# Sums with v stationary and a moving, long row loads from SyncE, v stored with partitions outermost, and one softmax product on GpSimd

## The chip, the cores and the metric

The kernel runs on one core of a Trainium2 chip. The metric is device time in microseconds, the median of several executions. In the tables PE is TensorE (matmuls), PEld its weight loads, DVE is VectorE, ACT is ScalarE, POOL is GpSimd and SP is SyncE, which here only issues transfers. "q" behind an engine's name is its instruction queue. A name such as L369 is line 369 of the kernel before.

## The reference

Attention through 32 memory slots for each of 8 batches and 8 heads (576 positions, head size 64), then a mixture of depths over the joined heads:

```
a   = softmax(phi, axis=slots)                  # (8, 8, 576, 32)
k_m = einsum('bhsm,bhsd->bhmd', a, k)
v_m = einsum('bhsm,bhsd->bhmd', a, v)           # "the sums"
x   = softmax(q k_m^T / 8) v_m                  # (8, 576, 512), heads joined
scores = x @ w_gate
for b: the 128 rows with the highest score get
    x += sigmoid(score) * (relu(x @ w1) @ w2)   # w1 512x1024, w2 1024x512
```

Which rows are chosen depends on small differences of the scores. So the kernel computes the softmax over the slots and the sums for v with more precision than one pass gives: a and v are split into a part of high bits and a remainder (hi and lo, by masking the low 12 bits), and the products of all parts are summed.

## The kernel before

**Softmax.** `softmax(i, ch)` works on one group of four heads of one batch, slots on the partitions: tiles of 128 x 576. There are 16 groups. It is a long chain of VectorE instructions with ScalarE roundings between them: a polynomial and a quotient, each step as `fma`, which multiplies in two parts. `fma` (L214 to L223) is called four times a group. Its `low = val * rl` is L221, and its addition L222 reads `low`. At the end `keys` transposes a (L306), splits it (L312, L314), writes its parts `alo` and `ahi` to the DRAM tensor `aparts` (L320, eight transfers a group, issued by POOL; L326 then copies them inside DRAM so that they stand there twice), and multiplies it with k (L330).

**v.** `split_v(b)` loads v in pieces of 128 x 1152 (L282), splits them into `vhi` and the remainder in `vb` (L285, L287), and stores each part twice in the DRAM tensor `vparts` (L290, four transfers a piece, issued by POOL, two buffers of each tile).

**The sums.** `values(st)` handles two batches (a set; there are four). In chunks of T = 16 positions it loads rows of vparts and aparts into `v_rows` and `a_rows` (two buffers; L350 by SP, L356 half by SP and half by POOL). A row of a chunk in a_rows consists of pieces of 32 floats. For each position four matmuls follow (L369), one for each strip of 32 partitions, into four accumulators: a is stationary (32 x 64), v moves (128 columns). The sums are evicted by ScalarE (L378), and `centre` transposes them (L392) and evicts them again (L394).

**The rest.** `attention(b)`: scores, exponentials, the product with v_m (L524), scaling (L528), a row added on POOL (L531), the gate's score (L498 to L503), the output (L535), the ranking and a gather (L600). `ffn` does two products with w1 and w2 (L625, L635) and scatters rows (L641).

**Order.** Each engine works through its instructions in the order in which the program gives them. That order is made by a loop of turns at the end of the kernel: a turn advances the softmaxes by one `yield`, v by one on every second turn while both chains run, the sums by STEPS = 9 (one yield is two positions), the attentions by one each, and a feed-forward by one or two. Two softmax chains run side by side until groups 0 to 7 are done; groups 8 to 15 form one chain. The sums of a set start 8 turns after its four groups.

Of the kernel before, what the change touches and what calls it, by code (L numbers as in the profile page):

```python
# [20 lines left out]
P = 128  # L21
# [17 lines left out]
def kernel(  # L39
# [27 lines left out]
    SET = 2  # L67
    T = 16
    scale = 1.0 / Dh ** 0.5
# [112 lines left out]
    def softmax(i, ch):  # L182
# [3 lines left out]
        def t(name, dtype=F32):  # L186
            return ex.tile([P, S], dtype, name=name)
# [26 lines left out]
        def fma(val, h, c):  # L214


            lo, big, low = t("lo"), t("big"), t("low")
            stt(out=lo, in0=val, scalar=GRID, in1=h, op0=ALU.mult, op1=ALU.subtract)  # L218
            tt(out=big, in0=h, in1=rh, op=ALU.mult)
            tt(out=lo, in0=lo, in1=rh, op=ALU.mult)  # L220
            tt(out=low, in0=val, in1=rl, op=ALU.mult)  # L221
            tt(out=low, in0=low, in1=lo, op=ALU.add)  # L222
            stt(out=val, in0=big, scalar=c * UP, in1=low, op0=ALU.add, op1=ALU.add)  # L223
# [54 lines left out]
    def split_v(b):  # L278

        for u in range(2):  # L280
            vb = vio.tile([P, S * Dh * NPR // P], F32, name="vb")
            nc.sync.dma_start(out=vb, in_=v[b, u])  # L282
            yield
            hi = vio.tile([P, S * Dh * NPR // P], F32, name="vhi")
            nc.vector.tensor_single_scalar(hi.bitcast(I32), vb.bitcast(I32), -4096,  # L285
                                           op=ALU.bitwise_and)
            nc.vector.tensor_sub(vb, vb, hi)  # L287
            for vp, src in enumerate((vb, hi)):
                for ap in range(2):
                    nc.gpsimd.dma_start(  # L290
                        out=vparts[u, b, :, ap, vp].rearrange("g r s d -> g (r s d)")
                                                   .rearrange("g (p x) -> g p x", p=P // 2),
                        in_=src)
            yield
# [3 lines left out]
    def keys(i, ch):  # L298
        ex, (b, g) = exs[ch], groups[i]
        a = soft.pop(i)  # L300
        kb = ks.pop(i)
        aS = ex.tile([PT, NC, P], F32, name="aS")
        for c0 in range(0, NC, 3):
            tp = bank([PT, 3, P])
            for c in range(3):
                nc.tensor.transpose(out=tp[:, c], in_=a[:, (c0 + c) * PT:(c0 + c + 1) * PT],  # L306
                                    identity=ident)
            nc.scalar.activation(aS[:, c0:c0 + 3], tp, AF.Copy)  # L308
        yield
# [6 lines left out]
        last = i == len(groups) - 1  # L316
        for h in range(4):
            for part, src in enumerate((lo, hi)):
                for vp in range(2 if last else 1):
                    (nc.sync if vp else nc.gpsimd).dma_start(  # L320
                        out=aparts[h // 2, h % 2, b, g, part, vp].rearrange("(c p) m -> p c m", p=PT),
                        in_=src[:, :, h * M:(h + 1) * M])
# [18 lines left out]
    def values(st):  # L341

        b0 = st * SET

        def load(ch):
            ss = slice(ch * T, (ch + 1) * T)
            for u in range(2):
                nc.sync.dma_start(  # L350
                    out=v_rows[ch % 2][2 * u::4, u].rearrange("p s d -> p (s d)").bitcast(F32),
                    in_=vparts[u, b0:b0 + SET].rearrange("b g t w r s d -> (b g t w r) (s d)")
                        [:, ch * T * Dh:(ch + 1) * T * Dh])
            for r in range(2):
                for u in range(2):
                    (nc.sync, nc.gpsimd)[u].dma_start(  # L356
                        out=a_rows[ch % 2][4 * r + 2 * u::8, :, r].bitcast(F32),
                        in_=aparts[r, u, b0:b0 + SET].rearrange("b g t w s m -> (b g t w) s m")[:, ss])

        n = S // T  # L360
        load(0)
        for ch in range(n):
            if ch + 1 < n:
                load(ch + 1)
            vr, ar = v_rows[ch % 2], a_rows[ch % 2]
            for s in range(T):
                for i in range(2 * SET):
                    p = slice(i * 32, i * 32 + 32)
                    nc.tensor.matmul(out=accs[i][:2 * M, :P].rearrange("p (u d) -> p u d", d=Dh),  # L369
                                     lhsT=ar[p, s].rearrange("p r m -> p (r m)"), rhs=vr[p, :, s],  # L370
                                     start=(ch == 0 and s == 0), stop=(ch == n - 1 and s == T - 1))
                if s % 2:
                    yield
        for bb in range(SET):
            v_m[b0 + bb] = const.tile([P, P], F32, name=f"v_m{b0 + bb}")
            for g in range(2):
                half = slice(g * 2 * M, (g + 1) * 2 * M)
                nc.scalar.activation(v_m[b0 + bb][half], accs[2 * bb + g][:2 * M, :P], AF.Copy)  # L378

    mean = {}  # L380

    def centre(b):
# [199 lines left out]
    def gather(b, t):  # L582
# [14 lines left out]
        gr = work.tile([P, 1], F32, name="gr")  # L597
        nc.scalar.activation(gr[:n], ps[:n, 1:2], AF.Tanh, scale=0.5)
        xe = work.tile([P, D], F32, name="xe")
        nc.gpsimd.indirect_dma_start(  # L600
# [6 lines left out]
    def ffn(b, t):  # L607
# [26 lines left out]
        for f in range(KF):  # L634
            nc.tensor.matmul(out=ps[:n], lhsT=hT[:, f, :n], rhs=w2_sb[:, f],  # L635
                             start=(f == 0), stop=(f == KF - 1))
            yield
        ye = one.tile([P, D], F32, name="ye")
        nc.vector.scalar_tensor_tensor(out=ye[:n], in0=ps[:n], scalar=gr[:n], in1=xe[:n],
                                       op0=ALU.mult, op1=ALU.add)  # L640
        nc.gpsimd.indirect_dma_start(  # L641
            out=out_flat[:(b + 1) * S],
            out_offset=bass.IndirectOffsetOnAxis(ap=idx[:n, 0:1], axis=0),
            in_=ye[:n], in_offset=None)

# [79 lines left out]

    STEPS = 9
    late_consts()
# [5 lines left out]
    while True:  # L733
# [77 lines left out]
```

## Time and profile before

| | before |
|---|---|
| median of 3 (range) | 1350.65 us (1348.28 to 1356.15) |
| span of the profiled execution | 1360.9 us |
| PE, PEld busy | 674.4 us, 479.3 us |
| DVE, ACT, POOL busy | 763.0 us, 292.6 us, 434.9 us |
| transfers | 166.41 MB in 201,868 packets, 154,896 of them under 512 B |
| sums' matmuls (L369) | 9,216, busy 245.5 us, from 346 us to 1,245 us |
| row loads issued on POOL (L356) | 288, busy 161.6 us |

How to read the profile: a line of the waits names the engine and instruction that waited, then what ended the wait, then the total in us, the number of times and the longest. A line of the groups has the busy time, the mean of one in ns and, behind the second bar, the engine's idle time just before them. A line of the busy times by stretch starts with the stretch in us and its length, then the busy us (and instructions) of PE, PEld, DVE, ACT and POOL, and last the granted TensorE clock, the share of the DMA engines and GB/s. A line of the timeline has the start and the duration in us. A line of the DMA issues has the count, KB each and the median us from issue to landing.

### The profile page before, as it was taken

Reading aid. Unit: us, or ns where it says so; the run is one execution under the profiler, and the core shown is the slowest. Engines: PE = TensorE matmul, PEld = TensorE weight load, DVE = VectorE, ACT = ScalarE, POOL = GpSimd, SP = SyncE. Lnnn points to the kernel's source line nnn. Section 1 sums busy time; section 2 is a strip of 40 time slices with the busy share of each in tenths; the row PEclk is TensorE's granted clock in tenths of the full one; section 3 lists DMA queues with packets and bytes.
Section 4 is the critical chain, followed back from the end, with each engine's and each line's share of the span. In section 5 each row is a group of like instructions: output and inputs, shape, how many; then the busy total and the mean of one; then the engine's idle time right before and its main releaser. Section 6 shows DMA issues by size and latency. Waiting matters only on the chain.

```text
span 1360.9 us, 25950 instructions
## 1 busy us (share of the span) xinstructions
PE 674.4 (50%) x10746; PEld 479.3 (35%) x10746; DVE 763.0 (56%) x1307; ACT 292.6 (21%) x569; POOL 434.9 (32%) x671
## 2 busy tenths in 40 slices
PE   0202010100336562474765645877464887677976
PEld 0101010100335452353553424555342555544542
DVE  8865846474434478375775876764937433202740
ACT  2202212121011213221413330421313220102320
POOL 5222313131423342325243234325230344321320
PEclk9999999999755655567668767776767778678968
DMA  8566767676555553344435244335440544433110
GB/s 274 150 159 180 186 159 178 128 185 180 133 128 118 126 139 94 98 120 124 124 104 141 73 109 124 96 96 159 99 108 12 117 136 126 110 94 76 67 42 18
DMA packets 201868, 166.41 MB, mean 122 GB/s; under 512 B 154896, under 2 KB 165136, under 8 KB 201744
## 3 DMA queue, kind: packets, MB, share of 16 engines
q0 software_dynamic: 88288, 79.37, 23.7%
q1 hardware_dynamic: 113456, 85.30, 23.6%
q8 instruction: 88, 1.44, 0.4%
q14 instruction: 36, 0.29, 0.1%
HBM read 105.05 MB, written 68.16 MB: 127 GB/s over the span
## 4 chain that ended last, share of the span: by engine, by line
DMA 32%; DVE 24%; PE 23%; POOL 6%; SPq 6%; issue 5%; ACT 3%; DVEq 0%; POOLq 0%; ACTq 0%
DMA a_rows<-aparts 13%; DMA vparts<-vhi 9%; PE acc L369 8%; DMA vparts<-vb 4%; SPq L350 4%; PE bank L625 3%; PE bank L635 3%; DMA vb<-in_v 3%; POOL aparts L320 2%; SPq L356 2%; DMA aparts<-alo 2%; PE bank L524 2%; DVE low L222 2%; DVE low L221 1%; DVE lo L218 1%
## 5 line engine op out<-in xcount | busy, mean ns | idle before, releaser
L369 PE MATMUL acc<-v_rows,a_rows 32*64 32x128 f32 x9216 | 245.5, 273 | 290.9 <-DMA a_rows<-aparts 286.2
L369 PEld LDWEIGHTS acc<-v_rows,a_rows 32*64 32x64 f32 x9216 | 220.4, 182 | 370.9 <-issue 277.3
L356 POOL DMA_DIRECT2D a_rows<-aparts x288 | 161.6, 567 | 410.1 <-PE acc L369 386.2
L306 PE MATMUL bank<-ident,e 128*96 128x128 f32 x96 | 23.7, 416 | 230.8 <-DVE e L273 230.3
L330 PE MATMUL bank<-aS,kb 96*128 96x64 f32 x384 | 70.8, 368 | 76.3 <-ACT aS L308 76.3
L306 PEld LDWEIGHTS bank<-ident,e 128*96 128x96 f32 x96 | 16.7, 191 | 238.5 <-issue 183.6
L330 PEld LDWEIGHTS bank<-aS,kb 96*128 96x128 f32 x384 | 69.8, 281 | 83.9 <-ACT aS L308 78.4
L625 PE MATMUL bank<-w_sb,xeT 128*128 128x512 f32 x128 | 87.9, 796 | 3.9 <-ACT xeT L616 3.9
L320 POOL DMA_DIRECT2D aparts<-alo x64 | 47.6, 743 | 128.9 <-DVE alo L314 86.9
L635 PE MATMUL bank<-w_sb,hT 128*128 128x512 f32 x128 | 81.6, 750 | 0.0
L290 POOL DMA_DIRECT2D vparts<-vb x32 | 26.0, 818 | 154.6 <-DVE vb L287 154.6
L285 DVE TENSOR_SCALAR vhi<-vb 128x1152 int32<-128x1152 int32 x16 | 12.3, 772 | 99.2 <-DMA vb<-in_v 56.6
L524 PE MATMUL bank<-vbd,eT 128*128 128x256 f32 x160 | 64.4, 542 | 0.0
L218 DVE SCALAR_TENSOR_TENSOR lo<-num,vh 128x576 f32<-128x576 f32 x48 | 36.1, 751 | 50.0 <-ACT vh L177 35.2
L498 DVE TENSOR_TENSOR prod<-xj,wg 128x1024 f32<-128x1024 f32 (+1 forms) x24 | 25.1, 1044 | 68.9 <-POOL xj L531 68.9
L531 POOL TENSOR_TENSOR xj<-xj,mean 128x1024 f32<-128x1024 f32 (+1 forms) x24 | 48.6, 2024 | 35.1 <-DVE xj L528 34.6
L177 ACT ACTIVATE vh<-num 128x576 int16<-128x576 f32 x32 | 21.9, 683 | 139.6 <-DVE num L223 130.8
L222 DVE TENSOR_TENSOR low<-low,lo 128x576 f32<-128x576 f32 x64 | 48.5, 758 | 2.2
L320 POOL DMA_DIRECT2D aparts<-ahi x64 | 47.5, 742 | 5.7 <-DMA vparts<-vb 2.2
L220 DVE TENSOR_TENSOR lo<-lo,rh 128x576 f32<-128x576 f32 x64 | 48.0, 750 | 0.0
L528 DVE TENSOR_TENSOR xj<-bank,rd 128x512 f32<-128x512 f32 x40 | 27.4, 687 | 35.7 <-PE bank L524 35.1
L524 PEld LDWEIGHTS bank<-vbd,eT 128*128 128x128 f32 x160 | 37.0, 256 | 17.9 <-issue 13.2
(151 smaller groups left out, 1294.7 us busy)
## 6 DMA issues: line engine op xcount, KB each, us to landing
v_rows<-vparts SPq DMA_DIRECT2D x288, 128.0 KB, 3.1
vparts<-vb POOLq DMA_DIRECT2D x32, 576.0 KB, 18.4
vparts<-vhi POOLq DMA_DIRECT2D x32, 576.0 KB, 20.8
kb<-in_k SPq DMA_DIRECT2D x16, 576.0 KB, 5.8
vb<-in_v SPq DMA_DIRECT2D x16, 576.0 KB, 8.0
a_rows<-aparts SPq DMA_DIRECT2D x288, 32.0 KB, 2.8
a_rows<-aparts POOLq DMA_DIRECT2D x288, 32.0 KB, 2.7
qb<-in_qT SPq DMA_DIRECT2D x16, 576.0 KB, 5.5
```

The costliest lines, as they stand in the source:

```text
L218: stt(out=lo, in0=val, scalar=GRID, in1=h, op0=ALU.mult, op1=ALU.subtract)
L220: tt(out=lo, in0=lo, in1=rh, op=ALU.mult)
L222: tt(out=low, in0=low, in1=lo, op=ALU.add)
L320: (nc.sync if vp else nc.gpsimd).dma_start(out=aparts[h // 2, h % 2, b, g, part, vp].rearrange("(c p) m -> p c m", p=PT), in_=src[:, :, h ...
L330: nc.tensor.matmul(out=km[:, rr], lhsT=kb[:, c, rr * P:(rr + 1) * P], rhs=aS[:, c, rr * 2 * M:(rr + 1) * 2 * M], start=(c == 0), stop=(c = ...
L350: nc.sync.dma_start(out=v_rows[ch % 2][2 * u::4, u].rearrange("p s d -> p (s d)").bitcast(F32), in_=vparts[u, b0:b0 + SET].rearrange("b g ...
L356: (nc.sync, nc.gpsimd)[u].dma_start(out=a_rows[ch % 2][4 * r + 2 * u::8, :, r].bitcast(F32), in_=aparts[r, u, b0:b0 + SET].rearrange("b g ...
L369: nc.tensor.matmul(out=accs[i][:2 * M, :P].rearrange("p (u d) -> p u d", d=Dh), lhsT=ar[p, s].rearrange("p r m -> p (r m)"), rhs=vr[p, :, ...
L524: nc.tensor.matmul(out=o[:, g * 4 * Dh:(g + 1) * 4 * Dh], lhsT=eT[:, g, (c0 + c) * P:(c0 + c + 1) * P], rhs=vbd[b % 3][:, g], start=False, ...
L531: nc.gpsimd.tensor_add(x, x, row.unsqueeze(1).to_broadcast([P, cols, D]))
L625: nc.tensor.matmul(out=ps[:n], lhsT=xeT[:, d, :n], rhs=w1_sb[:, d, f0:f0 + 512], start=(d == 0), stop=(d == KD - 1))
L635: nc.tensor.matmul(out=ps[:n], lhsT=hT[:, f, :n], rhs=w2_sb[:, f], start=(f == 0), stop=(f == KF - 1))
```

## The change

The sums exchange the roles of their operands: v is stationary (32 x 64), a's four heads move (4 x 32 columns). All loads of rows are issued by SP, in chunks of T = 24, with one run of 6 KB or 3 KB on a row; the doubled rows of a are read twice from one copy, so that `aparts` and its copies in DRAM shrink. A transpose and an eviction in `centre` fall away. v is handled by groups and stored with the partitions as outermost dimension, in two transfers a piece. The product `low` of each `fma` and v's subtraction move to POOL. The feed-forward writes its result into `xe` in place, with three buffers. One yield in `keys`, after the product with k, goes, and the turns are set anew. The tiles `gr` and `xe` get three buffers as `idx` does.

```diff
-    T = 16
+    T = 24
-    v_rows = [rows.tile([P, 2, T, Dh], F32R, name=f"v_rows{i}") for i in range(2)]
-    a_rows = [rows.tile([P, T, 2, M], F32R, name=f"a_rows{i}") for i in range(2)]
+    v_rows = [rows.tile([P, T, Dh], F32R, name=f"v_rows{i}") for i in range(2)]
+    a_rows = [rows.tile([P, 4, T, M], F32R, name=f"a_rows{i}") for i in range(2)]
...
+            nc.gpsimd.tensor_tensor(out=low, in0=val, in1=rl, op=ALU.mult)
             stt(out=lo, in0=val, scalar=GRID, in1=h, op0=ALU.mult, op1=ALU.subtract)
+            tt(out=lo, in0=lo, in1=rh, op=ALU.mult)
             tt(out=big, in0=h, in1=rh, op=ALU.mult)
-            tt(out=lo, in0=lo, in1=rh, op=ALU.mult)
-            tt(out=low, in0=val, in1=rl, op=ALU.mult)
             tt(out=low, in0=low, in1=lo, op=ALU.add)
...
-            nc.vector.tensor_sub(vb, vb, hi)
+            nc.gpsimd.tensor_sub(vb, vb, hi)
+            yield
             for vp, src in enumerate((vb, hi)):
-                for ap in range(2):
-                    nc.gpsimd.dma_start(
-                        out=vparts[u, b, :, ap, vp].rearrange("g r s d -> g (r s d)")
-                                                   .rearrange("g (p x) -> g p x", p=P // 2),
-                        in_=src)
+                nc.gpsimd.dma_start(
+                    out=vparts[b, g, :, vp].rearrange("w r s d -> w (r s d)")
+                                           .rearrange("w (p x) -> p w x", p=P),
+                    in_=src.unsqueeze(1).to_broadcast([P, 2, 4 * S * Dh // P]))
...
-        for part in range(0 if last else 2):
-            copies = aparts.rearrange("r u b g t w s m -> b g t w (r u) (s m)")[b, g, part]
-            copies = copies.rearrange("w h (x y) -> w x h y", x=16)
-            nc.gpsimd.dma_start(out=copies[1], in_=copies[0])
+        for part, src in enumerate((lo, hi)):
+            for h in range(4):
+                nc.gpsimd.dma_start(
+                    out=aparts[h, b, g, part].rearrange("(c p) m -> p c m", p=PT),
+                    in_=src[:, :, h * M:(h + 1) * M])
...
-        yield
...
+            nc.sync.dma_start(
+                out=v_rows[ch % 2][0::2].rearrange("p s d -> p (s d)").bitcast(F32),
+                in_=vparts[b0:b0 + SET].rearrange("b g t w r s d -> (b g t w r) (s d)")
+                    [:, ch * T * Dh:(ch + 1) * T * Dh])
+            for h in range(4):
+                src = aparts[h, b0:b0 + SET].rearrange("b g t s m -> (b g t) (s m)")
+                src = src[:, ch * T * M:(ch + 1) * T * M]
                 nc.sync.dma_start(
-                    out=v_rows[ch % 2][2 * u::4, u].rearrange("p s d -> p (s d)").bitcast(F32),
-                    in_=vparts[u, b0:b0 + SET].rearrange("b g t w r s d -> (b g t w r) (s d)")
-                        [:, ch * T * Dh:(ch + 1) * T * Dh])
-            for r in range(2):
-                for u in range(2):
-                    (nc.sync, nc.gpsimd)[u].dma_start(
-                        out=a_rows[ch % 2][4 * r + 2 * u::8, :, r].bitcast(F32),
-                        in_=aparts[r, u, b0:b0 + SET].rearrange("b g t w s m -> (b g t w) s m")[:, ss])
+                    out=a_rows[ch % 2][2 * h::8, h].rearrange("p s m -> p (s m)").bitcast(F32),
+                    in_=src.unsqueeze(1).to_broadcast([4 * SET, 2, T * M]))
...
-                    nc.tensor.matmul(out=accs[i][:2 * M, :P].rearrange("p (u d) -> p u d", d=Dh),
-                                     lhsT=ar[p, s].rearrange("p r m -> p (r m)"), rhs=vr[p, :, s],
+                    nc.tensor.matmul(out=accs[i][:Dh, :P].rearrange("p (h m) -> p h m", m=M),
+                                     lhsT=vr[p, s], rhs=ar[p, :, s],
...
-        tp = bank([P, P])
-        nc.tensor.transpose(out=tp, in_=v_m[b], identity=ident)
-        vm = work.tile([P, NPR, M], F32, name="vmT")
-        nc.scalar.activation(vm.rearrange("p r m -> p (r m)"), tp, AF.Copy)
+        vm = v_m[b]
...
-        idx = work.tile([P, 1], I32, name="idx")
+        idx = work.tile([P, 1], I32, name="idx", bufs=3)
...
-            for _ in range(8 * STEPS):
+            for _ in range(5 * STEPS):
...
-    STEPS = 9
+    STEPS = 7
...
-        for _ in range(STEPS):
+        for _ in range(STEPS + 2 * (not working)):
```

More of the change, by code (lines that the diff above doesn't have):

```diff
@@ L278, in split_v @@
     def split_v(b):
-        for u in range(2):
-            vb = vio.tile([P, S * Dh * NPR // P], F32, name="vb")
-            nc.sync.dma_start(out=vb, in_=v[b, u])
+        for g in range(NG):
+            vb = vio.tile([P, 4 * S * Dh // P], F32, name="vb")
+            nc.sync.dma_start(out=vb, in_=v[b, g])
             yield
-            hi = vio.tile([P, S * Dh * NPR // P], F32, name="vhi")
+            hi = vio.tile([P, 4 * S * Dh // P], F32, name="vhi")
             nc.vector.tensor_single_scalar(hi.bitcast(I32), vb.bitcast(I32), -4096,
                                            op=ALU.bitwise_and)
-            nc.vector.tensor_sub(vb, vb, hi)
+            nc.gpsimd.tensor_sub(vb, vb, hi)
+            yield
             for vp, src in enumerate((vb, hi)):
-                for ap in range(2):
-                    nc.gpsimd.dma_start(
-                        out=vparts[u, b, :, ap, vp].rearrange("g r s d -> g (r s d)")
-                                                   .rearrange("g (p x) -> g p x", p=P // 2),
-                        in_=src)
+                nc.gpsimd.dma_start(
+                    out=vparts[b, g, :, vp].rearrange("w r s d -> w (r s d)")
+                                           .rearrange("w (p x) -> p w x", p=P),
+                    in_=src.unsqueeze(1).to_broadcast([P, 2, 4 * S * Dh // P]))
             yield
@@ L314, in keys @@
         nc.vector.tensor_sub(lo, aS, hi)
[L316 to L322, printed above, removed]
-        for part in range(0 if last else 2):
-            copies = aparts.rearrange("r u b g t w s m -> b g t w (r u) (s m)")[b, g, part]
-            copies = copies.rearrange("w h (x y) -> w x h y", x=16)
-            nc.gpsimd.dma_start(out=copies[1], in_=copies[0])
+        for part, src in enumerate((lo, hi)):
[3 more added lines that the diff above has]
+                    in_=src[:, :, h * M:(h + 1) * M])
         km = bank([P, 2, 2 * M])
@@ L347, in load @@
         def load(ch):
-            ss = slice(ch * T, (ch + 1) * T)
-            for u in range(2):
-                nc.sync.dma_start(
-                    out=v_rows[ch % 2][2 * u::4, u].rearrange("p s d -> p (s d)").bitcast(F32),
-                    in_=vparts[u, b0:b0 + SET].rearrange("b g t w r s d -> (b g t w r) (s d)")
-                        [:, ch * T * Dh:(ch + 1) * T * Dh])
-            for r in range(2):
-                for u in range(2):
-                    (nc.sync, nc.gpsimd)[u].dma_start(
-                        out=a_rows[ch % 2][4 * r + 2 * u::8, :, r].bitcast(F32),
-                        in_=aparts[r, u, b0:b0 + SET].rearrange("b g t w s m -> (b g t w) s m")[:, ss])
+            nc.sync.dma_start(
[5 more added lines that the diff above has]
+                src = src[:, ch * T * M:(ch + 1) * T * M]
+                nc.sync.dma_start(
+                    out=a_rows[ch % 2][2 * h::8, h].rearrange("p s m -> p (s m)").bitcast(F32),
+                    in_=src.unsqueeze(1).to_broadcast([4 * SET, 2, T * M]))
         n = S // T
@@ L374, in values @@
         for bb in range(SET):
[L375 to L378, printed above, removed]
+            v_m[b0 + bb] = const.tile([P, NPR, M], F32, name=f"v_m{b0 + bb}")
+            for g in range(NG):
+                for u in range(2):
+                    nc.scalar.activation(
+                        v_m[b0 + bb][u * Dh:(u + 1) * Dh, 2 * g:2 * g + 2],
+                        accs[2 * bb + g][:Dh, :P].rearrange("p (r u m) -> p r u m", r=2, u=2)[:, :, u],
+                        AF.Copy)
     mean = {}
@@ L593, in gather @@
         yield
-        idx = work.tile([P, 1], I32, name="idx")
+        idx = work.tile([P, 1], I32, name="idx", bufs=3)
         nc.vector.tensor_scalar_add(idx[:n], ps[:n, 0:1], float(b * S))
-        gr = work.tile([P, 1], F32, name="gr")
+        gr = work.tile([P, 1], F32, name="gr", bufs=3)
         nc.scalar.activation(gr[:n], ps[:n, 1:2], AF.Tanh, scale=0.5)
-        xe = work.tile([P, D], F32, name="xe")
+        xe = work.tile([P, D], F32, name="xe", bufs=3)
         nc.gpsimd.indirect_dma_start(
@@ L637, in ffn @@
             yield
-        ye = one.tile([P, D], F32, name="ye")
-        nc.vector.scalar_tensor_tensor(out=ye[:n], in0=ps[:n], scalar=gr[:n], in1=xe[:n],
+        nc.vector.scalar_tensor_tensor(out=xe[:n], in0=ps[:n], scalar=gr[:n], in1=xe[:n],
                                        op0=ALU.mult, op1=ALU.add)
@@ L643, in ffn @@
             out_offset=bass.IndirectOffsetOnAxis(ap=idx[:n, 0:1], axis=0),
-            in_=ye[:n], in_offset=None)
+            in_=xe[:n], in_offset=None)
     def attention(b, general=False):
@@ L790 @@
               .reshape(B, H // 4, PT, NC, 4 * Dh),
-        "v": v.reshape(B, H // 2, 2, S, Dh).transpose(0, 2, 1, 3, 4).reshape(B, 2, P, -1),
+        "v": v.reshape(B, H // 4, P, -1),
         "phiT": phi.transpose(0, 1, 3, 2).reshape(B, H // 4, P, S),
@@ L804 @@
     out = nc.dram_tensor("out", (B, S, H * Dh), F32, kind="ExternalOutput").ap()
-    vparts = nc.dram_tensor("vparts", (2, B, H // 4, 2, 2, 2, S, Dh), F32, kind="Internal").ap()
-    aparts = nc.dram_tensor("aparts", (2, 2, B, H // 4, 2, 2, S, phi.shape[3]), F32, kind="Internal").ap()
+    vparts = nc.dram_tensor("vparts", (B, H // 4, 2, 2, 4, S, Dh), F32, kind="Internal").ap()
+    aparts = nc.dram_tensor("aparts", (4, B, H // 4, 2, S, phi.shape[3]), F32, kind="Internal").ap()
     with tile.TileContext(nc) as tc:
```

## The prediction

> **What bounds the kernel now.** I read the chain that ended last, then the waits, then busy time in stretches cut where the work changes. The chain, by engine and by line:
>
> ```profile
> DMA 32%; DVE 24%; PE 23%; POOL 6%; SPq 6%; issue 5%; ACT 3%; DVEq 0%; POOLq 0%; ACTq 0%
> DMA a_rows<-aparts 13%; DMA vparts<-vhi 9%; PE acc L369 8%; DMA vparts<-vb 4%; SPq L350 4%; PE bank L625 3%; PE bank L635 3%; DMA vb<-in_v 3%; POOL aparts L320 2%; SPq L356 2%; DMA aparts<-alo 2%; PE bank L524 2%; DVE low L222 2%; DVE low L221 1%; DVE lo L218 1%
> ```
>
> A third is transfers, of two kinds: v going out to vparts, and rows coming back for the sums. The waits of the whole run show the second kind as a loop: POOL and SP wait for PE to free a row buffer, PE waits for the rows.
>
> ```profile
> POOL a_rows L356 <- PE acc L369: 386.2, 101, 18.7
> PE acc L369 <- DMA a_rows<-aparts: 286.2, 78, 44.3
> ...
> POOL vparts L290 <- DVE vb L287: 154.6, 9, 34.8
> ```
>
> The waits of VectorE from 0 to 345 us, and those of the SP queue over the run, show the first kind: VectorE stands 99 us before v's split (L285), because SP may not reload vb until its store has landed.
>
> ```profile
> DVE vhi L285 <- DMA vb<-in_v: 56.6, 4, 22.7
> DVE vhi L285 <- DMA vparts<-vhi: 27.9, 1, 27.9
> DVE vhi L285 <- DMA aparts<-ahi: 14.7, 1, 14.7
> ```
> ```profile
> SPq L282 <- DMA vparts<-vb: 290.7, 14, 30.6
> ```
>
> Busy time by stretch: both softmax chains (0 to 521, the eighth group's alo), one chain (to 1060, the last alo), last sums (to 1245), rest.
>
> ```profile
> 0.00:521.00 521.00, 120.05 (x2538) 111.29 (x2539) 312.54 (x453) 101.81 (x164) 154.42 (x253) 0.87 0.65 162
> 521.00:1060.00 539.00, 318.69 (x5324) 224.84 (x5324) 355.90 (x640) 138.28 (x278) 186.75 (x285) 0.69 0.39 103
> 1060.00:1245.00 185.00, 143.89 (x2570) 94.99 (x2569) 43.82 (x101) 23.42 (x58) 67.68 (x103) 0.75 0.46 116
> 1245.00:1361.00 116.00, 91.81 (x318) 48.17 (x316) 50.70 (x115) 29.09 (x71) 26.10 (x30) 0.86 0.14 45
> ```
>
> After each stretch's length stand PE, PEld, DVE, ACT and POOL. VectorE is 60% and 66% busy in the first two, PE 78% and 79% in the last two. So the first two have room; the last two are mostly matmuls, which the change keeps.
>
> **What the Trainium skill says.**
> 1. "DMA: Bandwidth & Descriptors", section "Why a DMA increments its semaphore by 16 and not by 1": a DMA runs on the largest number of engines, up to 16, that divides the slowest dimension of both sides. The v store is 2x64x1152 on the DRAM side, so 2 engines for each of four DMAs. The trace agrees: from 28 to 40 us its packet records hold 8.2 packets in flight, each 4,608 B in 178 ns. The same bytes as kb take over three times as long to land:
>
> ```profile
> vparts<-vb POOLq DMA_DIRECT2D x32, 576.0 KB, 18.4
> vparts<-vhi POOLq DMA_DIRECT2D x32, 576.0 KB, 20.8
> kb<-in_k SPq DMA_DIRECT2D x16, 576.0 KB, 5.8
> ```
>
> 2. "SBUF — State Buffer", section "Who interferes with whom": a VectorE instruction with two SBUF inputs and a GpSimd instruction that reads SBUF lock each other out for a whole instruction. The trace agrees: a product of 0.8 us took 2.91 us behind xj on POOL (timelines of both engines).
>
> ```profile
> 682.40 0.75 DVE L220 TENSOR_TENSOR lo<-lo,rh 128x576 f32<-128x576 f32 x1
> 683.07 2.91 DVE L221 TENSOR_TENSOR low<-num,rl 128x576 f32<-128x576 f32 x1
> ```
> ```profile
> 682.80 2.56 POOL L531 TENSOR_TENSOR xj<-xj,mean 128x1024 f32<-128x1024 f32 x1
> ```
>
> 3. "GPSIMD Engine Reference", section "Performance versus the Vector engine": a two-input product costs about 2.6 cycles an element on GpSimd against 1. The trace's groups by form give 1,294 ns for 512 elements and 2,389 for 1,024, thus 2.14 ns each: 1.43 us for 576, 2.66 us for 1,152, which I use.
>
> **The change part by part.**
> - *v store.* Outermost dimension 128 on both sides, so I take 16 engines: two stores are 512 rows x 178 ns / 16 = 5.7 us of packets, where now the 8 engines take 11.4. With the lead seen now (issue 19.9, packets from 25) about 12 us to landing (8 to 20). A split now spans six turns, some 25 us, with two buffers: the 99 us of waits go.
> - *Product L221 to POOL (64).* VectorE loses 0.80 us, but POOL's 1.43 us locks out VectorE's neighbours, nearly all with two SBUF inputs. Serial: +0.63 each, 2.5 us a group. Hidden in VectorE's 0.8 us wait for vh (L177): -0.8 each. I take it serial.
> - *v's subtraction to POOL (16).* 2.66 instead of 1.36: +1.3 us each, serial.
> - *New wait.* VectorE's addition (L222) now waits for POOL, whose queue holds eight aparts issues a group (8 x 0.74 = 6 us). In the built program each also waits for the DMA issued eight before it, which can be a fresh v store; such waits are 34.4 and 11.6 us now and hurt nobody. Behind them stand the other chain's product and VectorE. I take 3 us a group (0 to 15).
> - *Row loads.* The 288 POOL issues (162 us) and POOL's 386 us behind PE go. SP issues five DMAs a chunk instead of four, but 96 chunks instead of 144. From freeing a buffer to the landing is now 5.2 us (median over the records of issue and landing), for 64 matmuls of 1.97 us; I take 6 us (5 to 8) for 96 matmuls of 2.95 us, with the same bytes a step but runs of 6 and 3 KB instead of 4 KB and 128 B (147,456 packets of 128 B go, 13 ns each). A chunk at its fastest is (6 + 2.95)/2 = 4.5 us, so a set falls from 36 x 3.6 = 129 to 24 x 4.5 = 107 us. The matmuls keep K = 32, M = 64, N = 128: no change.
> - *Gone from POOL:* 30 DRAM copies (16 us and 48 us of waits). In centre a transpose and an eviction go: small. Bufs of 3 and ye in place only ease waits; memsets at the start grow by half, 3 us.
> - *Order.* Turns carry the whole kernel. Counting yields: a group took 12 turns, now 11; both chains end at turn 94 instead of 102, the last group at 176 instead of 192. A set was 32 turns after 8 empty ones, now 41 after 5. The last sums end at turn 222, not 232.
>
> **Sum by stretch.**
> 1. Eight and a half groups: VectorE 312.5 - 27 (34 products) - 22 (subtractions) = 263, plus POOL's locks 34 x 1.43 + 16 x 2.66 = 91: 354. Start +3, queue 8 x 3 = 24, remaining gaps 19: 400 instead of 521. Set 0 has 41 turns of 4.2 us for its 107 us and fits.
> 2. 82 turns. Now, without sums, a turn takes 41 us / 10 = 4.1 (766 to 807) and with sums 6.1 and 6.9 (196 and 220 us / 32), so sums add 2.0 to 2.8 for 72 matmuls and a wait of 1.75 a chunk (125.7 / 72). Now 56 matmuls, and the other PE work of a chunk outlasts the load: about 1.2, plus 0.2 for the locks: 5.5 x 82 = 450 instead of 539. VectorE would be at 356 - 24 + 43 = 375, PE near 315: both fit.
> 3. 45 turns instead of 40, two thirds of them with the same 72 matmuls a turn as now (4.9 us), the rest lighter or empty: 190 instead of 185.
> 4. 116, PE-bound.
>
> Together 1,156; the profiled span stands 10 us over the median, so 1,145.
>
> **Rivals.**
> - *A, the forecast* (52%): about 1,145.
> - *B, locks and queue hide* (17%): POOL's products fall into VectorE's waits for ScalarE. Stretch 1 is 320, 2 at 4.75 a turn 390, then 175 and 115: 990. For it: VectorE waits for vh in nearly every product now. Against: two interleaved chains fill those waits, and VectorE has few one-input instructions.
> - *C, POOL's queue takes the place of the v wait* (22%): 10 us a group and later landings. Stretch 1 470, 2 at 6.2 a turn 508, then 200 and 118: 1,286. For it: POOL is now in every product's path. Against: its 386 us behind PE go, and v's stores land sooner.
> - *D, slower* (7%): v stores gain nothing and each group's eight issues wait out a store (20 us), so stretch 1 is 521 + 8 x 5; VectorE and PE then alternate in stretch 2: 7.2 x 82 = 590; 195 and 118: 1,454. Against: the packet records that show half the engines idle.
>
> **How the numbers follow.** A leads, so 1,145. The range runs from a little above B's figure to a little above C's, 1,010 to 1,310: it leaves out half of B, D and a tail of C, under 0.2 in all. Faster by over 0.5%: A, B and C less a few hundredths, 0.91; within 0.5%: 0.02; slower: 0.07.
>
> **What would show it.** Right: vparts landing near 12 us; no wait of L285 for vb; VectorE instructions near 2 us beside POOL's products; the last alo near 850; PE's waits for rows under 120 us. Wrong: vparts still near 18; VectorE waiting for POOL's low over 100 us; SP late with rows because kb or vb reloads stand ahead of them; stretches 3 and 4 longer.

## The result and the profile after

The changed kernel takes 1142.62 us (median of 4, 1141.73 to 1144.05) against 1352.99 us: a ratio of 0.845 (95% interval 0.842 to 0.848). The forecast was 1,145 us. The first two stretches, cut at the same events as before, came within 3 us of their forecasts; the third was to grow a little and shrank, the fourth was to stay and grew:

| stretch ends with | before | forecast | after |
|---|---|---|---|
| alo of the eighth group | 521 us | 400 us | 397 us |
| last alo | 539 | 450 | 449 |
| last sums | 185 | 190 | 173 |
| last instruction | 116 | 116 | 122 |

The busy times by stretch of the changed kernel (PE, PEld, DVE, ACT, POOL, then clock, DMA share, GB/s):

```profile
0.00:397.00 397.00, 103.59 (x2448) 95.56 (x2448) 321.37 (x403) 101.29 (x162) 174.16 (x181) 0.86 0.56 189
397.00:846.00 449.00, 263.44 (x4775) 187.75 (x4776) 365.86 (x590) 133.97 (x269) 149.77 (x153) 0.70 0.39 116
846.00:1019.00 173.00, 142.29 (x3185) 95.14 (x3184) 52.87 (x120) 28.10 (x72) 29.90 (x37) 0.88 0.47 140
1019.00:1141.00 122.00, 95.95 (x332) 49.98 (x330) 48.87 (x115) 31.84 (x76) 25.12 (x30) 0.88 0.14 43
```

VectorE is busy about as long as before in the first two stretches (321 and 366 us against 313 and 356), which are 214 us shorter; it is now 81% busy in both. That is not the same work: some 73 us of it have moved to POOL (64 products of 0.80 us and 16 subtractions of 1.36 us), and what is left takes longer. The chain that ended last has moved accordingly, from transfers (32%, now 5%) to VectorE (24%, now 49%):

```profile
DVE 49%; PE 21%; issue 9%; POOL 7%; DMA 5%; ACT 4%; SPq 3%; DVEq 0%; ACTq 0%; POOLq 0%
DVE lo L220 6%; PE acc L360 5%; DVE lo L219 5%; DVE low L222 4%; POOL aparts L317 4%; DMA a_rows<-aparts 3%; PE bank L616 3%; DVE num L223 3%; PE bank L626 3%; SPq L347 3%; DVE e L272 2%; DVE ph L198 2%; PE bank L323 2%; PE bank L515 2%; DVE cmp L563 2%
```

PE's wait for rows over the whole run is 129.2 us where it was 286.2:

```profile
PE acc L360 <- DMA a_rows<-aparts: 129.2, 46, 17.4
```

The DMA issues: a store of v carries twice the bytes of one before and lands in 4.8 or 7.4 us, where it took 18.4 or 20.8.

```profile
vparts<-vb POOLq DMA_DIRECT2D x16, 1152.0 KB, 4.8
vparts<-vhi POOLq DMA_DIRECT2D x16, 1152.0 KB, 7.4
```

VectorE's longest wait in the first stretch (waits of VectorE, 0 to 397 us) is no longer for v but for the product that moved:

```profile
DVE low L222 <- POOL low L218: 47.1, 7, 8.9
```

What such a wait looks like, in the timelines of POOL and of VectorE around 120 us (start, duration):

```profile
116.82 2.91 POOL L317 DMA_DIRECT2D aparts<-ahi  x4
119.74 1.41 POOL L218 TENSOR_TENSOR low<-num,rl 128x576 f32<-128x576 f32 x1
123.48 3.23 POOL L287 TENSOR_TENSOR vb<-vb,vhi 128x1152 f32<-128x1152 f32 x1 [2.33 <-DVE vhi L285]
```
```profile
121.18 0.76 DVE L222 TENSOR_TENSOR low<-low,lo 128x576 f32<-128x576 f32 x1 [5.48 <-POOL low L218]
...
124.28 3.05 DVE L220 TENSOR_TENSOR lo<-lo,rh 128x576 f32<-128x576 f32 x1
127.25 1.95 DVE L221 TENSOR_TENSOR big<-vh,rh 128x576 f32<-128x576 int16 x1
```

POOL is still issuing one group's aparts when the other chain needs its product; VectorE stands 5.5 us. Then POOL's subtraction runs, and a VectorE product of 0.75 us beside it takes 3.05.

So the total was right. Whether it was right for the stated reasons, the experiments decide: two parts of the change were forecast to cost time, and the others to gain more.

### The profile page after: what moved, and what is told of

It reads as the page before. It is cut to its first block, busy times and chain, and to the rows that moved or that the text cites. A ratio compares the mean times of both kernels' runs of the same rounds, so it can differ in the third digit from the quotient of the medians.

```text
span 1141.4 us, 25115 instructions
## 1 busy us (share of the span) xinstructions
PE 605.3 (53%) x10738; PEld 428.4 (38%) x10738; DVE 789.0 (69%) x1227; ACT 295.2 (26%) x577; POOL 378.9 (33%) x401
## 3 DMA queue, kind: packets, MB, share of 16 engines
q8 instruction: 87, 1.43, 0.5%
## 4 chain that ended last, share of the span: by engine, by line
DVE 49%; PE 21%; issue 9%; POOL 7%; DMA 5%; ACT 4%; SPq 3%; DVEq 0%; ACTq 0%; POOLq 0%
DVE lo L220 6%; PE acc L360 5%; DVE lo L219 5%; DVE low L222 4%; POOL aparts L317 4%; DMA a_rows<-aparts 3%; PE bank L616 3%; DVE num L223 3%; PE bank L626 3%; SPq L347 3%; DVE e L272 2%; DVE ph L198 2%; PE bank L323 2%; PE bank L515 2%; DVE cmp L563 2%
## 5 line engine op out<-in xcount | busy, mean ns | idle before, releaser
L360 PE MATMUL acc<-a_rows,v_rows 32*64 32x128 f32 x9216 | 221.0, 255 | 132.1 <-DMA a_rows<-aparts 129.2
L360 PEld LDWEIGHTS acc<-a_rows,v_rows 32*64 32x64 f32 x9216 | 196.3, 164 | 214.3 <-issue 120.0
L218 POOL TENSOR_TENSOR low<-num,rl 128x576 f32<-128x576 f32 x48 | 74.5, 1551 | 94.3 <-DVE num L223 72.5
L287 POOL TENSOR_TENSOR vb<-vb,vhi 128x1152 f32<-128x1152 f32 x16 | 47.3, 2955 | 139.5 <-DVE vhi L285 139.4
L220 DVE TENSOR_TENSOR lo<-lo,rh 128x576 f32<-128x576 f32 x64 | 80.9, 1264 | 2.2
L219 DVE SCALAR_TENSOR_TENSOR lo<-num,vh 128x576 f32<-128x576 f32 x48 | 55.6, 1158 | 16.4 <-ACT vh L177 16.1
L515 PE MATMUL bank<-vbd,eT 128*128 128x256 f32 x160 | 53.4, 463 | 0.0
L563 DVE SCALAR_TENSOR_TENSOR cmp<-row,tg,wide 128x576 bf16<-128x576 f32 x40 | 39.4, 985 | 10.0 <-ACT row L549 9.2
L198 DVE SCALAR_TENSOR_TENSOR ph<-q,ph 128x576 f32<-128x576 int16 x32 | 32.1, 1003 | 13.6 <-ACT q L177 13.0
L450 DVE SCALAR_TENSOR_TENSOR eT<-es,th 128x288 f32<-128x288 f32 x32 | 17.0, 530 | 35.4 <-ACT th L448 34.5
```

What stands on the lines that cost most here:

```text
L198: stt(out=r, in0=q, scalar=-ln2, in1=r, op0=ALU.mult, op1=ALU.add)
L218: nc.gpsimd.tensor_tensor(out=low, in0=val, in1=rl, op=ALU.mult)
L360: nc.tensor.matmul(out=accs[i][:Dh, :P].rearrange("p (h m) -> p h m", m=M), lhsT=vr[p, s], rhs=ar[p, :, s], start=(ch == 0 and s == 0), st ...
L515: nc.tensor.matmul(out=o[:, g * 4 * Dh:(g + 1) * 4 * Dh], lhsT=eT[:, g, (c0 + c) * P:(c0 + c + 1) * P], rhs=vbd[b % 3][:, g], start=False, ...
L563: nc.vector.scalar_tensor_tensor(out=cmp, in0=row, scalar=g, in1=wide[:, off:off + S], op0=ALU.is_equal, op1=ALU.mult, accum_out=equal[:, ...
```

## The experiments

Each run is given as the median and its ratio to the kernel before (95% interval), which ran on the same chip between them. The kernel before had medians of 1351 to 1357 us in these groups of runs, so a few us between two runs say nothing. Stretches are those of the one profiled execution of a run, which can lie some us off its median.

### The product and the subtraction back on VectorE

```diff
-            nc.gpsimd.tensor_tensor(out=low, in0=val, in1=rl, op=ALU.mult)
...
             tt(out=big, in0=h, in1=rh, op=ALU.mult)
+            tt(out=low, in0=val, in1=rl, op=ALU.mult)
```

> The changed kernel with the product low of fma back on VectorE, all else as changed. My theory: POOL's product costs more than it saves, since it locks VectorE out (VectorE's two-input instructions are 98 us longer than before in sum, about 70 of it beside these products) and VectorE waits 47 us more for it; VectorE gets 51 us of work back. Net 66 us less on VectorE, so about 1,090 us, and VectorE's lo and lo*rh back at 0.75 us. Rival: the product is hidden and moving it was a gain; then 1,170 us or more.

Measured: 1098.69 us, 0.810 (0.805 to 0.816).

```diff
-            nc.gpsimd.tensor_sub(vb, vb, hi)
+            nc.vector.tensor_sub(vb, vb, hi)
```

> The changed kernel with v's subtraction back on VectorE, all else as changed. My theory: 16 x 1.36 = 22 us come back to VectorE, about 28 us of locks go, and POOL's queue is 47 us shorter, so that VectorE waits less for low (47 us now, 25 then): about 1,120 us. Rival: moving it was a gain of 22 us: about 1,165 us.

Measured: 1116.60 us, 0.823 (0.818 to 0.828). VectorE's wait for low stays at 41 us (49 in the changed kernel), where I had expected 25: it is mostly the aparts issues that hold the product up. In the changed kernel's timelines three of the seven waits in the first stretch have nothing but these issues ahead of the product (5.5 us each); in two others the subtraction stands between as well (7.4 us each).

Both edits together:

> The changed kernel with both the product low and v's subtraction on VectorE. My theory: no locks and no waits for POOL, 73 us of work back against 98 + 47 us: about 1,075 us, less than either alone. Rival: both moves paid: about 1,190 us.

Measured: 1085.55 us, 0.801 (0.797 to 0.806). The busy time of its first two stretches, cut at the same events:

```profile
0.00:345.00 345.00, 109.31 (x2422) 101.40 (x2423) 314.34 (x451) 100.77 (x160) 78.99 (x133) 0.84 0.64 218
345.00:788.00 443.00, 252.73 (x4803) 181.79 (x4803) 360.53 (x621) 134.74 (x271) 95.82 (x121) 0.72 0.38 118
```

All three fell to the side of my theory. The two moves cost the changed kernel 57 us by the medians. The profiled executions lie 64 us apart (1077.0 and 1141.4), and 52 of these are in the first stretch (345 us instead of 397), where two chains keep VectorE 91% busy if it does the work itself. In the second stretch, with one chain, the moves cost little (449 us against 443). The locks are there too: 31 products and one subtraction, some 26 us of work, have left VectorE in that stretch, and its busy time there is still 5 us longer (365.9 us against 360.5). What the second stretch lacks is the wait for low, of whose 49 us 47 are in the first.

### The lock or the queue

```diff
-            nc.gpsimd.tensor_tensor(out=low, in0=val, in1=rl, op=ALU.mult)
+            for _ in range(3):
+                nc.gpsimd.memset(low, 0.0)
```

> The changed kernel with three memsets of low on POOL (some 1.6 us together) in the place of the product, which is left out: POOL is busy as long and VectorE waits for it as before, but POOL reads no SBUF. My theory: the lock alone costs some 70 us of VectorE's time, so lo and lo*rh fall back to 0.75 us and the time is about 1,090 to 1,110 us. Rival: the cost is the wait in POOL's queue, not the lock: then the time stays within 10 us of the changed kernel's 1,143 us.

Measured: 1101.24 us, 0.811 (0.806 to 0.816). The groups of this run:

```profile
L221 DVE TENSOR_TENSOR lo<-lo,rh 128x576 f32<-128x576 f32 x64 | 64.0, 1000 | 2.2
L223 DVE TENSOR_TENSOR low<-low,lo 128x576 f32<-128x576 f32 x64 | 48.2, 753 | 57.5 <-POOL low L219 57.4
L220 DVE SCALAR_TENSOR_TENSOR lo<-num,vh 128x576 f32<-128x576 f32 x48 | 39.6, 826 | 16.4 <-ACT vh L177 16.1
```

and of the changed kernel:

```profile
L220 DVE TENSOR_TENSOR lo<-lo,rh 128x576 f32<-128x576 f32 x64 | 80.9, 1264 | 2.2
L222 DVE TENSOR_TENSOR low<-low,lo 128x576 f32<-128x576 f32 x64 | 48.0, 750 | 49.3 <-POOL low L218 49.3
L219 DVE SCALAR_TENSOR_TENSOR lo<-num,vh 128x576 f32<-128x576 f32 x48 | 55.6, 1158 | 16.4 <-ACT vh L177 16.1
```

POOL's part takes as long (1.74 us for three memsets, 1.61 for the product) and VectorE waits for it as long (57 and 49 us), but POOL reads no SBUF, and VectorE's neighbours shrink: 1,158 ns to 826 for the first. The time falls by 41 us. VectorE's busy time over the run falls by 45 us (743.8 summed over the stretches, against 789.0), 22 us of it in the first stretch and 24 in the second. That is the lock, apart from the queue. The rest of lo*rh (1,000 ns) stays, as it does with the product on VectorE (1,008), and most of it is gone with both edits (820): it lies beside the subtraction.

### How many engines a store of v runs on

In the kernel before, each store cut in two:

```diff
-                    nc.gpsimd.dma_start(
-                        out=vparts[u, b, :, ap, vp].rearrange("g r s d -> g (r s d)")
-                                                   .rearrange("g (p x) -> g p x", p=P // 2),
-                        in_=src)
+                    for gg in range(NG):
+                        nc.gpsimd.dma_start(
+                            out=vparts[u, b, gg, ap, vp].rearrange("r s d -> (r s d)")
+                                                        .rearrange("(p x) -> p x", p=P // 2),
+                            in_=src[gg * (P // 2):(gg + 1) * (P // 2)])
```

> The kernel before with each v store cut in two along g, so that its DRAM side is 64 x 1152 and its outermost dimension 64 (eight transfers a piece instead of four); all else as before. My theory: they land in about 8 us instead of 18 to 20, the 99 us that VectorE stood before v's split up to 345 us go, and the rest of the stretch is held by VectorE and the sums: about 1,270 us. Rival: the bytes bound it and not the number of engines: about 1,350 us.

Measured: 1236.43 us, 0.915 (0.908 to 0.921). Its DMA issues, and the busy time of its first two stretches:

```profile
vparts<-vb POOLq DMA_DIRECT2D x64, 288.0 KB, 4.4
vparts<-vhi POOLq DMA_DIRECT2D x64, 288.0 KB, 5.8
```
```profile
0.00:405.00 405.00, 120.58 (x2540) 111.63 (x2541) 311.80 (x454) 101.79 (x164) 169.13 (x317) 0.83 0.70 207
405.00:940.00 535.00, 313.76 (x5322) 220.87 (x5322) 355.42 (x639) 137.98 (x277) 186.53 (x285) 0.69 0.39 104
```

The same bytes in the same runs, from twice as many transfers: 115 us less by the medians. The profiled executions lie 127 us apart, 116 of these in the first stretch (405 instead of 521). The packet records show the width: up to 16.2 packets in flight during a store (46 to 55 us), where the kernel before has 8.2. I had expected 83 us: the 99 us at v's split are gone, and VectorE's waits for ScalarE at ahi and lo, which I had not counted, fall from 86 to 71 us in that stretch as well.

The other way round, in the changed kernel. A first attempt, four transfers a piece with the DRAM side written as 2 x 64 x 1152:

> The changed kernel with v's store as before in shape: four transfers a piece whose DRAM side is 2 x 64 x 1152, all else as changed. My theory: each store lands in 18 to 20 us again instead of 5 to 7.5; since a split now spans six turns with two buffers, VectorE waits little for vb, but POOL's aparts issues wait for fresh stores and VectorE waits for low behind them: about 40 us more, 1,180 us. Rival: the wide store is most of the gain of the first stretch, which returns to about 520 us: 1,260 us.

Measured: 1139.34 us, 0.844 (0.838 to 0.850), with vb landing in 4.1 us. It tells nothing of the width: the two halves are adjacent in DRAM, so the built program has them as one dimension of 128. It does show that four transfers instead of two cost nothing. With padding between the halves the dimension of 2 stays:

```diff
-                nc.gpsimd.dma_start(
-                    out=vparts[b, g, :, vp].rearrange("w r s d -> w (r s d)")
-                                           .rearrange("w (p x) -> p w x", p=P),
-                    in_=src.unsqueeze(1).to_broadcast([P, 2, 4 * S * Dh // P]))
+                for w in range(2):
+                    nc.gpsimd.dma_start(
+                        out=vparts[b, g, w, vp][:, :2 * S * Dh].rearrange("h (p x) -> h p x", p=P // 2),
+                        in_=src)
...
-    vparts = nc.dram_tensor("vparts", (B, H // 4, 2, 2, 4, S, Dh), F32, kind="Internal").ap()
+    vparts = nc.dram_tensor("vparts", (B, H // 4, 2, 2, 2, 2 * S * Dh + 128), F32, kind="Internal").ap()
```

> The changed kernel with v's halves padded apart in DRAM, so that each store is 2 x 64 x 1152 on the DRAM side, four transfers a piece, as in the kernel before (in the earlier run with four transfers the two outer dimensions were one run and the store kept its outermost 128). My theory: the store lands in 18 to 20 us; a split spans six turns with two buffers, so VectorE hardly waits for vb, but POOL's aparts issues wait for fresh stores with products behind them: about 40 us more than the changed kernel, 1,180 us. Rival: the slower pace of the splits alone hides a slow store: 1,143 us within 10. Second rival: the first stretch returns to 520 us: 1,260 us.

Measured: 1202.46 us, 0.890 (0.884 to 0.896). DMA issues, then waits of VectorE, then waits of POOL:

```profile
vparts<-vb POOLq DMA_DIRECT2D x32, 576.0 KB, 18.6
vparts<-vhi POOLq DMA_DIRECT2D x32, 576.0 KB, 19.8
```
```profile
DVE low L222 <- POOL low L218: 101.8, 9, 18.6
...
DVE vhi L285 <- DMA vb<-in_v: 21.1, 2, 16.8
```
```profile
POOL aparts L317 <- DMA vparts<-vb: 48.8, 12, 11.6
```

The slow store is back, with 8 packets in flight, and 60 us with it; the first stretch is 56 us longer (453 us). Little of that is the old wait (21 us at vhi, 4 of them in the first stretch): POOL's aparts issues wait for stores, and VectorE's wait for the product behind them doubles, from 49 to 102 us. This is the coupling of rival C, and the wide store is what keeps it small.

One thing goes with the width that no run takes apart: a split's narrow stores come with some 3,600 packets of 4 bytes on POOL's queue, wide ones in two transfers with 32. How much of the slow landing is theirs is not shown.

### Row loads

Two of a chunk's four loads of a on POOL again:

```diff
-                nc.sync.dma_start(
+                (nc.sync, nc.gpsimd)[h % 2].dma_start(
                     out=a_rows[ch % 2][2 * h::8, h].rearrange("p s m -> p (s m)").bitcast(F32),
```

> The changed kernel with two of a chunk's four loads of a's rows issued by POOL, as half were before; all else as changed. My theory: 192 issues of about 0.57 us and their waits for PE stand in POOL's queue ahead of the products that VectorE needs, so VectorE waits for PE through POOL: 1,220 us or more. Rival: SP's queue is the narrower one (five issues of 0.6 us a chunk) and halving a's part there saves time: 1,130 us or less.

Measured: 1199.39 us, 0.887 (0.879 to 0.895), 57 us more. Waits of the run:

```profile
PE acc L360 <- DMA a_rows<-aparts: 250.0, 50, 43.1
...
POOL a_rows L347 <- PE acc L360: 225.8, 45, 24.2
```

POOL stands behind PE again, and VectorE's wait for low grows from 49 to 81 us, 32 of the 57 us. PE's waits for rows rise as well, from 129 to 250 us; the third stretch, where PE is busiest, is the same to 1 us (174). So with products on POOL, row loads in its queue cost time. What taking them away does without such products, a run of the kernel before was to show:

```diff
-                    (nc.sync, nc.gpsimd)[u].dma_start(
+                    nc.sync.dma_start(
```

> The kernel before with all row loads issued by SP (six a chunk of 16 positions), all else as before. My theory: POOL's 386 us behind PE go and with them VectorE's waits for POOL's xj (69 us), but POOL is not on the softmax's path here and SP issues two more a chunk, some 1.2 us of latency each: about 1,330 us. Rival: the loop through POOL holds the sums back by itself: below 1,280 us.

Measured: 1382.69 us, 1.022 (1.014 to 1.031): slower. My expectation fell. POOL's waits behind PE are gone, but the rows come later; waits of this run:

```profile
PE acc L369 <- DMA a_rows<-aparts: 307.6, 101, 38.0
```

(286.2 before). So removing POOL's 386 us of waiting, the longest line of the waits before, is no gain by itself. Two causes are mixed in this run. SP has six issues a chunk of 16 positions; and the packets change, which I had overlooked: the loads that POOL issued moved in 4,608 packets of 2 KB, those of SP in pieces of 128 B, so that the 128-byte packets go from 78,336 to 152,064. Which of the two makes the rows late is not shown; the changed kernel has neither, with five issues a chunk of 24 and packets of 6 and 3 KB. How much the length of a chunk is worth:

```diff
-    T = 24
+    T = 16
```

> The changed kernel with T = 16, so 144 chunks of 64 matmuls with five loads each instead of 96 of 96; all else as changed. My theory: a chunk's loads take as long to arrive and hide less behind its matmuls; PE's waits for rows rise from 129 to about 200 us, mostly in the last two stretches: about 1,170 us. Rival: the sums are not on the path and only the long runs mattered: 1,143 us within 10.

Measured: 1196.07 us, 0.887 (0.880 to 0.894), 53 us more. The waits of the run:

```profile
PE acc L360 <- DMA a_rows<-aparts: 211.3, 84, 17.0
```

39 of the 53 us lie in the third stretch (212 instead of 173 us), where PE is busiest (82% in the changed kernel), and 14 in the second. The edit also shortens the runs, to 4 and 2 KB, and raises the loads from 480 to 720: the 53 us are for all three together. Unbroken runs with the old chunk are thus not enough. The runs in a_rows alone (128 B again) weren't tried, nor the exchange of the operands alone.

### The turns

```diff
-    STEPS = 7
+    STEPS = 9
...
-            for _ in range(5 * STEPS):
+            for _ in range(8 * STEPS):
...
+        yield
...
-        for _ in range(STEPS + 2 * (not working)):
+        for _ in range(STEPS):
```

> The changed kernel with the old turns: the yield in keys back, STEPS 9 throughout, 8 empty turns before a set, all else as changed. My theory: the last sums end at turn 232 instead of 222 and a turn holds 72 matmuls instead of 56 while the softmaxes run; 1,160 to 1,180 us. Rival: the new turns are the main gain: above 1,230 us.

Measured: 1134.36 us, 0.838 (0.831 to 0.844): not slower, against expectation. Busy time by stretch:

```profile
0.00:401.00 401.00, 112.06 (x2543) 104.37 (x2543) 311.51 (x405) 102.24 (x168) 176.22 (x184) 0.86 0.59 199
401.00:884.00 483.00, 296.70 (x5315) 212.56 (x5315) 368.82 (x609) 138.58 (x280) 147.22 (x156) 0.71 0.35 105
884.00:1029.00 145.00, 120.96 (x2568) 82.69 (x2568) 45.62 (x100) 23.39 (x58) 27.98 (x31) 0.87 0.47 144
1029.00:1140.00 111.00, 91.61 (x316) 48.29 (x314) 50.67 (x115) 29.13 (x72) 26.09 (x30) 0.87 0.15 47
```

The first stretch is nearly the same (401 us against 397) though a group has 12 turns in it instead of 11. The second takes 34 us more and the third 28 less: 4,608 of the sums' matmuls instead of 4,120 fall into the second. The last takes 11 less (111 against 122). A turn of the second stretch takes 483 / 90 = 5.4 us with 72 matmuls and 449 / 82 = 5.5 us with 56, and I took from this that the matmuls of a turn do not lengthen it. The two turns are not alike, though: 90 turns share out the softmax work of 82, so each has a twelfth less of it. The run does not show what 16 matmuls cost.

Still, it suggested a better version, which compares turns of one kind: product and subtraction on VectorE, the short turns, and 9 yields throughout.

```diff
-    STEPS = 7
+    STEPS = 9
...
-        for _ in range(STEPS + 2 * (not working)):
+        for _ in range(STEPS):
```

> The changed kernel with the product low and v's subtraction on VectorE (1,086 us) and 9 yields of the sums a turn throughout instead of 7 and then 9; 5 empty turns and no yield in keys, as changed. My theory, from the run with the old turns, where a turn with 72 matmuls took no longer than one with 56: the last sums end nine turns earlier and some of their matmuls move into the stretch where PE has room: about 1,060 us. Rival: the last stretch is bound by PE and the others pay: 1,085 us or more.

Measured: 1068.44 us, 0.790 (0.784 to 0.796). It is faster than both kernels, and 17 us faster than with the two edits alone (0.790 against 0.801, two intervals that just miss each other; the profiled executions show 9 us of it). Its stretches take 357, 453, 140 and 118 us against 345, 443, 168 and 121. So with 82 turns in both second stretches, 16 more matmuls a turn cost 10 us there, 0.1 us a turn; the first stretch pays 12 and the third gains 28.

## Why the prediction was right

The main mechanisms were right: wide stores and a slower pace of the splits end the waits for v, longer runs and chunks shorten the waits for rows, and the moves to POOL cost time. That the total came within 3 us is luck. The stretches were forecast to sum to 1,156 us and take 1,141: the first, second and fourth are 3 and 1 us shorter and 6 longer, the third 17 shorter. The 10 us that I took off the sum, since the profile before lay that far over its median, have no counterpart after (a span of 1141.4 us, a median of 1142.6), and happen to make up for most of that. Inside the stretches, too, terms were off and made up for each other.

- **The v store: mechanism right, landing time too long.** I took 12 us (the 5 us lead seen before, plus 5.7 us of packets, plus an end) and it is 4.8 and 7.4. The packet records show up to 16.2 in flight from 33 to 37 us, as the Trainium skill's rule on engines ("DMA: Bandwidth & Descriptors", section "Why a DMA increments its semaphore by 16 and not by 1") says for an outermost 128. The 5 us lead was that of the first store of the kernel before, whose second starts after 1.5 us already; the first four pieces of the changed kernel have their first data packets 1.3 to 1.5 us after the issue. The v waits went as forecast: one of 6 us is left. The padded run, with 21 us, shows that the slower pace alone takes most of them; there the narrow store costs its time through POOL's queue. The width alone is worth 115 us in the kernel before and 60 in the changed one.
- **Product on POOL: sign right, terms mis-sized.** Serial, the product's locks would be 64 x 1.43 = 91 us. The memset run puts them at 45, and VectorE's instructions beside a product, forecast near 2 us, take 1.16 and 1.26 us on average (lo and lo*rh, 0.75 before). The prediction had the product either serial or hidden in VectorE's 0.8 us wait for vh; the timelines show it in part hidden: at 37.6 us a product of 1.40 us starts on POOL, VectorE waits 0.81 us for vh meanwhile, and then takes 1.28 us for lo. How much of the missing half this explains was not measured. That the memsets, which take POOL as long but only write, leave lo at 0.83 us agrees with what the Trainium skill states ("SBUF — State Buffer", section "Who interferes with whom"): a GpSimd instruction that only writes SBUF does not contend with a VectorE instruction of two SBUF inputs. The wait for low is 49 us, 47 of it in the first stretch, where I took 24 us for the queue; it comes about once a group, behind the eight aparts issues, at 5.5 to 8.9 us. Locks and waits, 94 us, less 51 us of work saved: 43 us lost; putting it back gains 44.
- **Subtraction on POOL: right.** 16 x 1.3 = 21 us lost was the term; putting it back gains 26.
- **First stretch.** VectorE is busy for 321 us, not 354 (locks smaller), waits 47 us for POOL, not 24, and stands for 29 us otherwise, not 22: 397 instead of 400. The errors have opposite signs, so this match is luck as well.
- **Second stretch.** VectorE 366 us busy (375 taken) and 5.5 us a turn as taken. But fewer matmuls a turn are little of the reason: the 1.2 us that I took for 56 would give 0.34 us for 16 matmuls if it went by their number, and at equal turns 16 cost 0.1 us. What shortened the turn from 6.0 to 5.5 us (539 / 90 before) was not isolated further than this: with row loads on POOL, or chunks of 16, the stretch takes 473 and 463 us, so those two hold part of it.
- **Order.** "The last sums end at turn 222, not 232" brought nothing measurable: with the old turns the kernel is not slower. The fourth stretch was to stay at 116 us and takes 122, with the old turns 111.
- **Row loads.** PE's wait for rows was to fall under 120 us and is 129. The third stretch was to grow to 190 and is 173: 45 turns cost 3.8 us each, less than the 4.9 of before that I carried over. Longer chunks do more where PE is busiest than I gave them: 39 us of that stretch by the run with T = 16. The count of 147,456 packets of 128 B that go is twice too high: only the half of the row loads that SP issued moved in such pieces. And one sign of being wrong came in part: SP stands 157 us (55 before) until kb may be reloaded (behind PE), with row loads behind it in the queue; how much of PE's 129 us that is, no run shows.
- **Rivals.** B (all hides) failed: it put the first two stretches at 320 and 390 us, and even with both moves undone they take 345 and 443. C (POOL's queue replaces the wait) is what the first would be with a narrow store: 453 us against C's 470.
- **Left open.** With both moves undone the changed kernel is 151 us under the kernel before with wide stores (1085.55 against 1236.43). The chunk of 24 with its longer runs may hold up to 53 of these; the exchange of the operands, the copies in DRAM that go and the slower pace of v's split were not run alone.

## What to carry to other kernels

Look at the outermost dimension of a store before its bytes: cutting each store in two, so that each runs on more engines, took 115 us off this kernel without touching its arithmetic. Before moving an elementwise instruction to an idle engine, ask what its neighbours read and what stands in that engine's queue: POOL was 32% busy, and two moves to it cost 57 us, because VectorE was locked out and waited behind transfer issues. The longest line of the waits (POOL, 386 us) was no bottleneck: moving these loads to another queue made the kernel slower. Before moving a transfer to another queue, count its packets there: the same loads went from pieces of 2 KB to pieces of 128 B.

## What was not expected of the hardware

- How much the outermost dimension of a store is worth: 1,152 KB land in 4.8 to 7.4 us, while 576 KB with an outermost 2 take 18.6 to 19.8 us beside their three fellows, in the same kernel but for the padding. It is not a later start: the first data packets of the padded stores, too, come some 1.5 us after the issue.
- 16 more matmuls of 128 columns in a turn of 5.4 us lengthened it by 0.1 us only (453 instead of 443 us for 82 turns, with product and subtraction on VectorE).
- The same row load of 32-float pieces moved in packets of 2 KB when POOL issued it and in packets of 128 B when SP did.
